# An earlier first AV in a fused attention and GELU kernel, with a weight load and a key load issued ahead of the weighing of v

## The chip, the cores and the metric

One core of one Trainium2 chip. The metric is the device time of one execution in microseconds (us); a "run" is one timed execution. Engines are named as in the profile: PE = TensorE, DVE = VectorE, ACT = ScalarE, POOL = GpSimd, SP = SyncE (which here only issues DMAs). The granted clock is the share of full speed at which the profile shows TensorE's clock; a load lands when its last byte has arrived. AV is the product of the exps with v.

## The reference

Attention with a decay that depends on `f`, over 8 batches of 8 heads (576 rows of 64), and then two matrix products with an exact GELU between them.

```python
def _attn_ref(q, k, v, f):                      # q, k, v: (8, 8, 576, 64)
    scores = scale * np.matmul(q, k.transpose(0, 1, 3, 2))
    cum = np.cumsum(np.log(np.clip(f, 0.0001, 1.0)), axis=-1)
    scores = np.where(causal, -1e9, scores + cum[:, :, :, None] - cum[:, :, None, :])
    ... softmax ...
    return np.matmul(attn, v)
def _moe_ref(x, w_in, w_out):                   # x: (4608, 512), d_ff = 2048
    h = x @ w_in
    return (0.5 * h * (1.0 + erf(h / sqrt(2)))) @ w_out
```

## The kernel before

The program is scheduled by hand: each engine executes its instructions in the order of the code. Batch 0's attention comes first, then its product with `w_in` (the "GEMM stream", line L385). Batch 1's attention follows, with parts of batch 0's `w_out` product (L517) as filler, and so on for each batch. Three jobs lie on GpSimd: it issues the loads of q, k, `w_in` and `w_out` (they convert to bf16), multiplies v by the decay ("weighing", four calls a batch, one for each pair of heads), and cuts the causal triangle out of the exps ("masks"). v is loaded by SyncE, batch 1's in two halves of four heads and five pieces each.

```python
def load_v(b, h0=0, h1=H):                       # L119, SyncE's queue
    for n in range(NBLK):
        p0 = D if n == NBLK - 1 else 0
        nc.sync.dma_start(v_sb[p0:P, h0:h1, n, :], v[b, h0:h1, ...])
def load_w_out(c):                               # L175, GpSimd's queue
    nc.gpsimd.dma_start(w_out_sb[:, kt, :], w_out_r[:, kt, :])
def weigh_v(b, i, eng=nc.gpsimd):                # L268: vw = v * w, heads 2i, 2i+1
    eng.tensor_tensor(vw(b)[:, hs, :, 0:D], v_sb[:, hs, :, :], w..., Alu.mult)
def scores(b, i, t):                             # L299 matmuls, then
    nc.scalar.activation(et[:, :, z:c], st[:, :, z:c], Act.Exp, scale=scale)   # L309
    for c0 in [] if on_pe else SDIAG[t]:         # on_pe: batch 0, and pair 0 of batch 1
        nc.gpsimd.affine_select(...)             # L311, a mask
# attend(b, i, h): AV, L330.   gemm1: the stream on w_in, L385.
# ... cut ...
def second_attention():                          # batch 1
    weigh_v(1, 2)
    weigh_v(1, 3)
    for i in range(HP):
        for t in range(4):
            scores(b, i, t)
            # ... transposes of q and k (i == 0), w_out filler (i > 1) ...
            if i and t in (1, 2):
                av(i - 1, t - 1)
            if (i, t) == (1, 3):
                load_qk_tokens(2, which="k")
    # ... cut ...
    load_w_out(2); load_w_out(3)
    load_v(2)
# in batch 0's GEMM stream:
if ffb == 12:
    weigh_v(1, 0)
    load_w_out(0); load_w_out(1)
    weigh_v(1, 1)
    load_qk_tokens(2, which="q")
```

The softmax here doesn't subtract the row's maximum and nothing guards it: scores larger than these inputs give would overflow.

## Time and profile before

| | before |
|---|---|
| time, first three runs | 344.74 us (343.18 to 345.57) |
| time, with the three runs beside the changed kernel | 343.41 us (342.94 to 345.57) |
| span of the profiled execution, granted clock | 343.5 us, 0.996 |
| long GEMM streams of batch 0 and 1 start | 25.60, 59.41 us |
| first AV of batch 2; last stream of matmuls starts | 84.49, 323.94 us |

A timeline line is: start, length, engine, line of the code, operation, output and inputs, and in brackets the idle time before and what ended it. These are GpSimd's weighings of batch 1, the w_out issue between them, and then TensorE's AV of batch 1's second pair and its GEMM stream:

```profile
39.42 1.28 POOL L268 TENSOR_TENSOR vw<-v_sb,wT 128x640 bf16<-128x640 f32 x1 [12.60 <-DMA v_sb<-in_v_dram]
40.79 1.56 POOL L175 DMA_DIRECT2D w_out_sb<-in_moe_w_out_dram  x2
...
44.58 1.29 POOL L268 TENSOR_TENSOR vw<-v_sb,wT 128x640 bf16<-128x640 f32 x1
```
```profile
49.18 0.64 PE L330 MATMUL o<-vw,e 128*128 128x65 bf16 x15
...
59.41 13.21 PE L385 MATMUL ps<-xT,w_in_sb 128*128 128x512 bf16 x60
```

The third weighing, at 44.58, has no bracket: GpSimd came to it without waiting. It reads v's second half, whose last piece the chain of waits shows (start, length, what):

```profile
36.90 4.98 DMA v_sb<-in_v_dram
```

It was issued at 36.90 and landed at 41.88, so 2.7 us before it was needed.

### The profile page before, as it was taken

The numbers are of one execution on the slowest core, as the hardware profiler recorded it, in microseconds if no ns is written. First come the engines' busy times: TensorE is split into PE (matmuls) and PEld (weight loads), VectorE is DVE, ScalarE is ACT, GpSimd is POOL, SyncE is SP. The second block draws the span as 40 slices with busy tenths as digits, with TensorE's granted clock in tenths as the row PEclk, the third lists the DMA queues.
The fourth block names the chain that finished last, engine by engine and source line by source line (L and its number), as shares of the span: only waits on it lengthen the run. The fifth ranks groups of instructions, "written<-read, shape, count | busy, mean of one in ns | idle before, by whom it ended". The sixth has DMA issues, their size and how long they took to land.

```text
span 343.5 us, 7832 instructions
## 1 busy us (share of the span) xinstructions
PE 332.4 (97%) x3172; PEld 172.6 (50%) x3172; DVE 184.7 (54%) x417; ACT 210.3 (61%) x299; POOL 121.9 (35%) x247
## 2 busy tenths in 40 slices
PE   8799999999999999999999999999999999999993
PEld 3574555445554456445644564456544654444442
DVE  4670355664457935796479646964696450010021
ACT  6986786773643787368737873787378746305500
POOL 8180492208634244623454343624352420000000
PEclk9999999999999999999999999999999999999998
DMA  8999999995998999398949698679900240020022
GB/s 117 177 175 194 160 178 129 134 210 119 220 200 207 140 180 199 101 137 125 232 121 132 117 200 168 86 132 205 164 31 2 88 85 31 0 93 32 0 61 63
DMA packets 104628, 44.18 MB, mean 129 GB/s; under 512 B 83408, under 2 KB 100048, under 8 KB 104592
## 3 DMA queue, kind: packets, MB, share of 16 engines
q1 hardware_dynamic: 87296, 29.52, 44.8%
q0 software_dynamic: 16896, 13.63, 27.5%
q8 instruction: 25, 0.41, 0.5%
q10 hardware_dynamic: 400, 0.52, 0.4%
q14 instruction: 11, 0.09, 0.1%
HBM read 36.85 MB, written 9.44 MB: 135 GB/s over the span
## 4 chain that ended last, share of the span: by engine, by line
PE 72%; SPq 11%; DMA 7%; POOL 6%; issue 1%; DVE 1%; POOLq 0%
PE ps L385 28%; PE ps L479 24%; SPq L119 9%; PE ps L421 8%; PE o L330 7%; PE s L299 5%; DMA v_sb<-in_v_dram 3%; DMA k<-in_k_dram 3%; POOL vw L268 2%; SPq L235 2%; POOL q L107 1%; POOL e L311 1%; DMA xT<-x 1%; POOL k L107 1%; DVE x L344 0%
## 5 line engine op out<-in xcount | busy, mean ns | idle before, releaser
L405 ACT ACTIVATE g<-ps 128x512 bf16<-128x512 f32 x144 | 82.1, 601 | 82.2 <-PE ps L385 82.0
L309 ACT ACTIVATE e<-s 128x896 bf16<-128x896 f32 (+2 forms) x128 | 101.2, 835 | 27.4 <-PE s L299 25.4
L385 PE MATMUL ps<-xT,w_in_sb 128*128 128x512 bf16 x512 | 112.7, 379 | 0.2 <-DMA xT<-x 0.2
L479 PE MATMUL ps<-w_out_sb,g 64*128 64x512 bf16 (+1 forms) x736 | 108.5, 377 | 0.0
L385 PEld LDWEIGHTS <-w_in_sb 128*128 128x128 bf16 x576 | 55.9, 98 | 68.0 <-issue 2.3
L311 POOL TENSOR_SCALAR_AFFINE_SELECT e<-e 128x256 bf16<-128x256 bf16 (+1 forms) x135 | 49.0, 383 | 90.6 <-ACT e L309 90.1
L479 PEld LDWEIGHTS <-g 64*128 64x128 bf16 (+1 forms) x736 | 41.9, 95 | 39.7 <-issue 8.9
L268 POOL TENSOR_TENSOR vw<-v_sb,wT 128x640 bf16<-128x640 f32 x30 | 39.2, 1308 | 37.4 <-DMA v_sb<-in_v_dram 29.2
L299 PE MATMUL s<-qT,kT 64*128 64x320 bf16 (+4 forms) x384 | 45.8, 277 | 3.7 <-ACT e L309 3.2
L249 DVE COPY qT<-tq 64x288 bf16<-64x288 bf16 x96 | 42.2, 440 | 4.0 <-DMA tq<-q 2.6
L249 DVE COPY kT<-tk 64x288 bf16<-64x288 bf16 x96 | 40.9, 426 | 4.9 <-DMA tk<-k 3.4
L487 DVE COPY ot<-ps 128x512 f32<-128x512 f32 x25 | 17.3, 691 | 41.7 <-PE ps L479 41.7
L330 PEld LDWEIGHTS <-e 128*128 128x128 bf16 x960 | 34.4, 98 | 7.4 <-POOL e L311 3.0
L330 PE MATMUL o<-vw,e 128*128 128x65 bf16 x960 | 37.3, 194 | 0.2 <-POOL e L311 0.2
L344 DVE TENSOR_TENSOR x<-o,r 128x320 bf16<-128x320 f32 x64 | 31.5, 491 | 2.2
L430 DVE COPY ot<-ps 128x512 f32<-128x512 f32 (+2 forms) x9 | 5.7, 633 | 48.9 <-PE ps L421 48.9
L299 PEld LDWEIGHTS <-kT 64*128 64x128 bf16 x384 | 19.6, 94 | 23.8 <-issue 10.5
L421 PE MATMUL ps<-w_out_sb,g 128*128 128x512 bf16 (+2 forms) x144 | 28.0, 356 | 0.0
L343 DVE RECIPROCAL r<-o 128x5 f32<-128x5 f32 x64 | 12.1, 190 | 22.8 <-PE o L330 22.6
L421 PEld LDWEIGHTS <-g 128*128 128x128 bf16 x144 | 13.5, 98 | 14.5
L490 DVE TENSOR_TENSOR ot<-ot,ps 128x512 f32<-128x512 f32 x25 | 17.2, 687 | 1.4
L216 DVE COPY qT<-ps_f 128x576 bf16<-128x576 bf16 x7 | 5.3, 754 | 17.3 <-PE ps_f L207 17.3
(64 smaller groups left out, 147.3 us busy)
## 6 DMA issues: line engine op xcount, KB each, us to landing
out_dram<-ot SPq DMA_DIRECT2D x32, 256.0 KB, 2.6
v_sb<-in_v_dram SPq DMA_DIRECT2D x24, 256.0 KB, 5.2
q<-in_q_dram POOLq DMA_DIRECT2D x6, 576.0 KB, 6.1
k<-in_k_dram POOLq DMA_DIRECT2D x6, 576.0 KB, 8.1
v_sb<-in_v_dram SPq DMA_DIRECT2D x22, 128.0 KB, 5.5
w_in_sb<-in_moe_w_in_dram POOLq DMA_DIRECT2D x4, 512.0 KB, 7.9
w_out_sb<-in_moe_w_out_dram POOLq DMA_DIRECT2D x4, 512.0 KB, 8.4
q<-in_q_dram POOLq DMA_DIRECT2D x4, 144.0 KB, 4.4
```

Of the source, the lines that this page charges most:

```text
L119: nc.sync.dma_start(v_sb[p0:P, h0:h1, n, :], v[b, h0:h1, K0[n] + p0 : K0[n] + P].rearrange("h p d -> p h d"),)
L249: nc.vector.tensor_copy(rows[:, odd], src[odd * D : (odd + 1) * D, 2 * i + h].rearrange("d j p -> d p j"),)
L268: eng.tensor_tensor(vw(b)[:, hs, :, 0:D], v_sb[:, hs, :, :], w.unsqueeze(3).to_broadcast([P, 2, NBLK, D]), Alu.mult,)
L299: nc.tensor.matmul(to, *ab, start=half < 0, stop=half == 1 or not masked)
L309: nc.scalar.activation(et[:, :, z:c], st[:, :, z:c], Act.Exp, scale=scale)
L311: nc.gpsimd.affine_select(out=et[:, :, c0 + z : c0 + P], in_=et[:, :, c0 + z : c0 + P], compare_op=Alu.is_ge, fill=0.0, base=z, pattern=[[ ...
L330: nc.tensor.matmul(o[:, m, :], e_of[b, i, t][:, h, c : c + P], vw_of[b][:, 2 * i + h, n, :], start=(n == 0), stop=(n == m),)
L344: nc.vector.tensor_tensor(x_of[b, i][:, :, h, :], o[:, :, 0:D], r.unsqueeze(2).to_broadcast([P, NBLK, D]), Alu.mult,)
L385: nc.tensor.matmul(ps, w_in_sb[:, kt, ffb * P : (ffb + 1) * P], src[:, kt, 0:TC], start=(kt == 0), stop=(kt == n_dm - 1),)
L405: nc.scalar.activation(g_of[c][ffb], ps, Act.Gelu)
L421: nc.tensor.matmul(pss[ts][:, c0:c1], g_of[c][kt][:, ts * P : (ts + 1) * P], w_out_sb[:, kt, c0:c1], start=(kt == 0), stop=(kt == n_ff - 1),)
L479: nc.tensor.matmul(banks[r], g_of[c][kt][rows, ts * P : (ts + 1) * P], w_out_sb[rows, kt, :], start=kt == (steps.index("r") if r else 0), ...
```

## The change

Its intent: keep TensorE busy in batch 0's attention by mixing the part that ScalarE paces with the part that TensorE paces, and bring batch 1's and batch 2's data in early enough for the time gained. Part 1 changes only the order in the first attention (one 128x640 copy goes from ScalarE to VectorE). Part 2 moves loads: w_out's first half behind a gate on a piece of v's first half and ahead of the first weighing, k of batch 2 next to q, and w_out's second half ahead of the end of batch 1's scores. A gate is a GpSimd copy of 64x1 out of a piece of v: GpSimd waits in it until that piece has landed, and so does all that follows it in GpSimd's order.

```diff
+    def gate(h, n):
+        t = x_pool.tile([P, 1], FP32, tag="gate", name="gate")
+        nc.gpsimd.tensor_copy(t[D:P], v_sb[D:P, h, n, 0:1])
 # part 1: first_attention (cut)
-        for t in (1, 2, 3):
-            scores(0, 1, t)
+        scores(0, 1, 1)
+        scores(0, 1, 2)
+        transposes_first(0, 3, 0, m_psum, "m")
+        scores(0, 1, 3)
+        transposes_first(0, 3, 1, m_psum, "m")
+        weigh_v(0, 0, nc.vector)
+        weigh_v(0, 1, nc.vector)
+        gate(0, 4)
-        scores(0, 2, 0)          # and the transposes and weighings, now above
-        for t in range(4):
-            scores(0, 3, t)
-            attend_head(*divmod(t, 2))
+        for i, t in ((2, 2), (2, 3), (3, 0), (3, 1), (3, 2), (3, 3)):
+            scores(0, i, t)
+            attend_head(*heads.pop(0))
 # part 2: second_attention, and batch 0's stream
-                if (i, t) == (1, 3):
-                    load_qk_tokens(2, which="k")
+                if (i, t) == (3, 3):
+                    load_w_out(2)
+                    load_w_out(3)
-        load_w_out(2)
-        load_w_out(3)
         load_v(2)
                 if ffb == 12:
-                    weigh_v(1, 0)
+                    gate(0, 2)
                     load_w_out(0)
                     load_w_out(1)
+                    weigh_v(1, 0)
                     weigh_v(1, 1)
-                    load_qk_tokens(2, which="q")
+                    load_qk_tokens(2)
```

More of the change, by code (lines that the diff above doesn't have):

```diff
@@ L576, in first_attention @@
         transposes(2, m_psum, "m")
-        for t in (1, 2, 3):
-            scores(0, 1, t)
-        gate = x_pool.tile([P, 1], FP32, tag="gate", name="gate")
-        nc.gpsimd.tensor_copy(gate[D:P], v_sb[D:P, 0, 4, 0:1])
+        scores(0, 1, 1)
[6 more added lines that the diff above has]
+        gate(0, 4)
         load_w_in(0)
@@ L584, in first_attention @@
         weigh_v(0, 3)
-        scores(0, 2, 0)
-        transposes_first(0, 3, 0, m_psum, "m")
-        scores(0, 2, 1)
-        transposes_first(0, 3, 1, m_psum, "m")
-        weigh_v(0, 0, nc.vector)
-        weigh_v(0, 1, nc.vector)
         load_w_in(2)
@@ L597, in first_attention @@
         load_qk_tokens(1, 4, 8)
-        scores(0, 2, 2)
-        scores(0, 2, 3)
-        for t in range(4):
-            scores(0, 3, t)
-            attend_head(*divmod(t, 2))
-        attend_head(2, 0)
-        to_xT(0, 0, nc.scalar.copy)
-        attend_head(2, 1)
+        scores(0, 2, 0)
+        scores(0, 2, 1)
+        heads = [(i, h) for i in range(3) for h in range(2)]
+        for i, t in ((2, 2), (2, 3), (3, 0), (3, 1), (3, 2), (3, 3)):
+            scores(0, i, t)
+            attend_head(*heads.pop(0))
+        to_xT(0, 0, nc.vector.tensor_copy)
         to_xT(0, 1, nc.scalar.copy)
```

## The prediction

> **What bounds the kernel now.** I read the page's busy line first, then TensorE's timeline of the first 110 us with its idle times, then ScalarE's and GpSimd's timelines beside it, and the chain of work that ended last.
>
> ```profile
> PE 332.4 (97%) x3172; PEld 172.6 (50%) x3172; DVE 184.7 (54%) x417; ACT 210.3 (61%) x299; POOL 121.9 (35%) x247
> ```
>
> TensorE (PE) is busy for 97% of a 343.5 us span and nothing else passes 61%. From 86 us on the chain is TensorE almost alone, and the change touches nothing there, so those 257 us stay and arrive earlier or later as a block. What can be won lies in front of 86 us, and is at most TensorE's idle and stalled time there. The first attention is one such place. These are its lines in TensorE's timeline (start, length, what, and in brackets the idle time before it), then the exps in ScalarE's:
>
> ```profile
> 10.93 0.29 PE L299 MATMUL s<-qT,kT 64*128 64x256 bf16 x2 [0.40 <-ACT e L309]
> 13.41 0.31 PE L299 MATMUL s<-qT,kT 64*128 64x320 bf16 x2 [0.49 <-ACT e L309]
> 14.22 0.29 PE L299 MATMUL s<-qT,kT 64*128 64x256 bf16 x2 [0.41 <-ACT e L309]
> 17.42 0.28 PE L299 MATMUL s<-qT,kT 64*128 64x256 bf16 x2 [0.56 <-ACT e L309]
> ...
> 20.64 1.28 PE L330 MATMUL o<-vw,e 128*128 128x65 bf16 x30
> ...
> 25.31 0.45 PE L363 MATMUL ps_x<-key_of,x 128*128 128x128 bf16 x5
> 25.60 12.35 PE L385 MATMUL ps<-xT,w_in_sb 128*128 128x512 bf16 x56
> ```
> ```profile
> 8.48 11.21 ACT L309 ACTIVATE e<-s 128x896 bf16<-128x896 f32 x14
> 19.84 1.61 ACT L309 ACTIVATE e<-s 128x896 bf16<-128x896 f32 x2 [0.15 <-PE s L299]
> ```
>
> The reader is to see two regimes: until about 17.4 us ScalarE's 16 exps set the pace (some 0.8 us each, back to back) and TensorE waits for a score buffer; after that TensorE is saturated, with four heads of AV left over behind the last exp (20.64 to 24.4), until the long GEMM stream at 25.60. Further on, GpSimd (POOL) sets TensorE's time twice:
>
> ```profile
> 47.34 1.72 POOL L311 TENSOR_SCALAR_AFFINE_SELECT e<-e 128x256 bf16<-128x256 bf16 x5
> 49.01 0.82 POOL L107 DMA_DIRECT2D k<-in_k_dram  x1
> ```
> ```profile
> 73.94 4.64 DMA v_sb<-in_v_dram
> 78.75 1.28 POOL vw L268
> 80.20 1.21 POOL vw L268
> 81.58 0.76 POOL q L107
> 82.33 0.76 POOL k L107
> 83.10 1.73 POOL e L311 x5
> 84.88 0.97 PE o L330 x25
> ```
>
> The first is GpSimd's timeline: the five masks of batch 1's second pair end at 49.0, and TensorE starts the AV that reads them at 49.18, so there is only some 0.2 us of slack. The second is the chain: batch 2's v lands at 78.7, its weighing, the issue of batch 3's q and k and five masks follow, and TensorE's AV stalls for it (30 matmuls take 1.36 us at 84.49, 1.11 us at 90.03: 0.25 us lost). The same chain runs back through the transposes of batch 2's k to its load, issued at 49.01 and landed at 58.3.
>
> **What the Trainium skill says.** Perfetto Trace Analysis, section "Optimization Strategy": where the most contended engine changes over time, interleave the regimes. That is the first part of the change, and the trace agrees that there are two (ScalarE's to 17.4 us, TensorE's after). SBUF — State Buffer, section "Who interferes with whom": a VectorE instruction with two SBUF inputs contends with a GpSimd instruction that reads SBUF, and the second to issue blocks. The trace agrees: GpSimd's first weighing, beside VectorE's at 17.56, took 1.87 us, and 1.28 us elsewhere. DMA: Bandwidth & Descriptors, section "Queues, rings and completion order": the engines round-robin between queue rows and take one ring's descriptors in order. So I take q, k, w_in and w_out (all from GpSimd's queue) as one line, beside v and the transposes (SyncE's). The landings fit: w_out at 46.5 and 48.7, q at 53.5, k at 58.3.
>
> **Part 1, the first attention.** No work is added or removed: it is the order, and one 128x640 copy (0.7 us on ScalarE, 0.49 on VectorE) changes engine. I replay TensorE with the durations of the timeline: scores 0.46, 0.30, 0.38 and 0.33 us for the four tiles, a transpose group 0.49, a head's AV 0.58 between scores, 0.56 otherwise, xT 0.3; a score may start 0.16 after the exp before last has gone (17.42 after 17.26), and an exp starts 0.45 after its scores.
> - The transposes of the last pair (2 x 0.49) go to 12.9 and 13.74. They fill the idle 0.49 and 0.41 there; the scores at 13.41 and 14.22 keep their places.
> - The first score of pair 2 stays at 14.22, the second goes to 14.95, the third waits for an exp until 15.76 and ends at 16.14.
> - The first AV needs VectorE's weighing. v lands at 15.4 (issued 8.20, 7.2 to landing; GpSimd's gate on it fires at 15.50), VectorE is free by 15.1, a weighing takes 0.82: so AV at 16.35, after 0.2 us of waiting.
> - Then six pairs of score and AV, 0.95 us each: scores at 16.93, 17.84, 18.88, 19.76 and 20.72. The exps slip: the last starts at 21.17 (20.75 before) and ends at 21.87.
> - Behind: AV of pair 2's second head to 21.61, two xT to 22.25, AV to 22.81, xT, AV to 23.66, four GEMM matmuls to 24.52, and the last xT 0.98 after the last AV as before: 24.64 against 25.31.
> So part 1 brings the GEMM stream forward by **0.67 us**: the 1.46 us of idle that it fills, less the 0.8 or so that it newly waits ahead of and after pair 2's scores.
>
> **Part 2, the loads.** Alone, part 1 would be lost at both of GpSimd's pins. Between v's landing (39.24) and the first mask GpSimd has now: four weighings with their casts 5.6 us, two w_out issues 1.56, one q issue 0.83, sum 7.99, which is 47.3. The change puts w_out behind a gate on an earlier piece of v (its third piece lands at 35.0), so 1.56 goes, and k's issue (0.82) comes in: the masks start 0.74 earlier, 46.55, and end at 48.3. TensorE, 0.67 ahead, wants them at 48.51. It fits. k of batch 2 is then issued near 43.2 in place of 49.0; w_out starts in the idle DMA stretch (40 to 44 us: mean busy share 0.48), lands some 4 us earlier, and q and k take 4.8 us each behind it: k lands at 54.6 (estimate) against 58.3. SyncE's transposes and v follow it, so v of batch 2 lands near 75 against 78.7. w_out's second half, issued at 56.5 in place of 60.5, takes some of that. Three microseconds are left, more than the 0.67 needed, and the stall of **0.25 us** at 84.5 goes too.
> Sum: 0.67 + 0.25 = 0.92 us at best.
>
> **The rivals.**
> - GpSimd is blocked by VectorE's weighing. Gate and weighing now wait for the same landing at 15.4, both read SBUF, and VectorE is idle. If it goes first, w_in's issue comes 0.8 us later, and with it the whole saturated stretch of DMA up to batch 1's v at 39.24 (now 40.0). The masks then end at 49.0 and TensorE stalls 0.5 us there: the gain is 0.2 + 0.25, time 344.3. Against it: the second weighing on VectorE no longer delays GpSimd's own (0.6 us back). About even with the main line.
> - v stays late. w_out and k move only from one end of a saturated queue to the other (DMA share 1.1 to 1.5 from 44 to 56 us), v of batch 2 does not come earlier, and the pin at 84.9 holds: nothing gained, 344.7. Against it is the idle DMA at 40 to 44 and 58 to 60 us.
> - The w_out loads, issued while batch 1's q, k and v still come in (landings 37.7 to 41.9), delay them; the transposes at 41.5 would wait. One to two microseconds lost, 346. Against it: one ring in order, so w_out stands behind q and k.
> - More is won: AV and scores overlap better than in my replay, all 1.46 us are saved and the stall too: 343.0.
>
> **Range and chances.** Mean of main line (0.9) and first rival (0.45), with the tails on both sides nearly even: 0.7 to 0.8 us off 344.74, so 343.9. Single runs of before lie between 343.18 and 345.57, so a median of few runs moves by about a microsecond by itself; hence 342.5 to 345.0. Two per cent is 6.9 us, more than TensorE's whole idle time before 86 us (88 less 82.7, 5.3 us), so faster is nearly ruled out; slower would need a stall several times any I see. Chances: faster 0.01, same 0.98, slower 0.01.
>
> **What would show it.** The gap of 0.56 at 17.42 and those of 0.49 and 0.41 gone; the first AV near 16.35; the last exp's end near 21.9; the GEMM stream's start near 24.9; w_in's issue at 15.96 (main line) or 16.8 (first rival); batch 1's masks ending before 48.5, without a wait of TensorE; k landing before 56, v of batch 2 before 76; no stall in the first AV of batch 2; the stretch from there to the end equal to before. A GEMM stream earlier by 0.6 with the same end would prove me wrong on part 2; a start at 25.3 or later, on part 1.

## More of the kernel before

A weighing of pair 0 or 1 reads the first half, of pair 2 or 3 the second.

In the view of the DMA queues from 36 to 40 us, q1 is SyncE's queue and q0 GpSimd's; the columns are packets, MB and the time their packets took as a share of 16 engines (packets overlap, so a sum over 100% is possible):

```profile
q1 hardware_dynamic: 2226, 0.55, 71.9%
q0 software_dynamic: 472, 0.34, 54.1%
```

w_out is not yet issued in this stretch, and v (q1) gets the larger part of the engines.

## The result, and the profile after

All outputs are correct. Each ratio in this document is the mean time of one kernel's fast runs over the mean of the other's from the same rounds, so it is not quite the ratio of the medians quoted.

| | before | after |
|---|---|---|
| median of six runs | 343.41 us (342.94 to 345.57) | 348.84 us (345.93 to 350.55) |
| ratio, 95% interval | | 1.0137 (1.0088 to 1.0186) |
| long GEMM stream of batch 0 starts | 25.60 | 24.68 |
| AV of batch 1's second pair (bulk of it) | 49.18 | 53.10 |
| long GEMM stream of batch 1 starts | 59.41 | 65.44 |
| first AV of batch 2 | 84.49 | 90.53 |
| last stream of matmuls starts | 323.94 | 329.59 |

The change cost some 5 us instead of winning 0.8. TensorE's timeline after:

```profile
24.68 12.35 PE L385 MATMUL ps<-xT,w_in_sb 128*128 128x512 bf16 x56
...
52.14 0.29 PE L330 MATMUL o<-vw,e 128*128 128x65 bf16 x2 [3.67 <-POOL e L311]
53.10 1.09 PE L330 MATMUL o<-vw,e 128*128 128x65 bf16 x13 [0.67 <-POOL e L311]
...
65.44 13.21 PE L385 MATMUL ps<-xT,w_in_sb 128*128 128x512 bf16 x60
...
90.53 1.11 PE L330 MATMUL o<-vw,e 128*128 128x65 bf16 x30
```

Two things are new. TensorE is idle for 3.67 and 0.67 us, waiting for GpSimd's masks. And behind the wait the matmuls are slow: 13 AV matmuls take 1.09 us, where 15 took 0.64. The account of the profiled executions, by the table above: +3.92 us up to the AV (0.92 gained in front already counted in), +2.11 from there to the GEMM stream (12.34 us against 10.23), +0.01 in the stream, and -0.39 behind batch 2's first AV, 0.25 of it the stall that the prediction wanted gone (30 matmuls now take 1.11 us, not 1.36). The sum is 5.65, close to the 5.43 between the medians.

Why the masks are late, in GpSimd's timeline after:

```profile
36.82 0.18 POOL L546 COPY gate<-v_sb 64x1 f32<-64x1 f32 x1 [10.93 <-DMA v_sb<-in_v_dram]
37.29 1.50 POOL L175 DMA_DIRECT2D w_out_sb<-in_moe_w_out_dram  x2 [0.28 <-issue]
...
44.46 0.78 POOL L107 DMA_DIRECT2D k<-in_k_dram  x1
48.93 1.28 POOL L268 TENSOR_TENSOR vw<-v_sb,wT 128x640 bf16<-128x640 f32 x1 [3.68 <-DMA v_sb<-in_v_dram]
...
51.68 2.68 POOL L311 TENSOR_SCALAR_AFFINE_SELECT e<-e 128x256 bf16<-128x256 bf16 x8
```

w_out is issued at 37.29, 3.5 us earlier than before. The third weighing, which never waited, now waits 3.68 us for v's second half, and the masks stand behind it in GpSimd's order. The masked pair itself does not need that half: the AV at 52.14 is of pair 1, whose v was weighed by the second weighing. The chain of waits names the piece:

```profile
38.56 10.21 DMA v_sb<-in_v_dram
```

The same 64 KB piece took 4.98 us before and takes 10.21 us now; it was also issued 1.66 us later, and lands at 48.77 in place of 41.88. The DMA queues from 40 to 44 us, after:

```profile
q0 software_dynamic: 597, 0.59, 89.2%
q1 hardware_dynamic: 977, 0.24, 32.8%
```

GpSimd's queue (w_out, then q) takes most of the engines' time with packets of about 1 KB (0.59 MB in 597), and v's packets of about 0.25 KB (0.24 MB in 977) move at less than half of the 0.55 MB in 4 us that they reached before.

The slow matmuls behind the wait are seen in the windows of 2 us. Columns: stretch, length, busy time and instructions of PE, PEld, DVE, ACT and POOL, granted clock of TensorE, DMA share, GB/s:

```profile
52.00:54.00 2.00, 1.18 (x15) 0.86 (x15) 0.00 (x0) 0.00 (x0) 2.00 (x7) 0.50 1.15 148
54.00:56.00 2.00, 2.00 (x18) 0.97 (x16) 0.69 (x2) 0.92 (x1) 0.60 (x3) 0.50 0.59 106
56.00:58.00 2.00, 2.00 (x17) 0.67 (x14) 0.69 (x2) 0.70 (x1) 0.45 (x2) 0.50 0.97 175
```

The granted clock is 0.50 from about 51.2 to 58.0 us; before, it is 1.00 throughout this stretch. Before and after:

```profile
52.00:54.00 2.00, 2.00 (x28) 1.14 (x25) 0.62 (x2) 1.70 (x3) 1.12 (x3) 1.00 1.12 160
```
```profile
48.00:50.00 2.00, 0.46 (x2) 0.00 (x0) 0.18 (x1) 0.86 (x2) 1.07 (x1) 1.00 1.31 206
50.00:52.00 2.00, 0.00 (x0) 0.00 (x0) 0.00 (x0) 0.00 (x0) 2.00 (x5) 0.80 1.33 205
```

The Trainium skill, TensorE: Matmul & The Clock Gate, section "What's actually happening", says that the clock halves after an idle window of about 3.4 us and comes back after about as much busy time. This trace agrees only in part. (A mean of 0.80 from 50 to 52 is full clock until 51.2 and half clock after; windows of 0.25 us say the same.) The half clock lasted 6.8 us, twice that window. But it began some 2.75 us after the end of the last matmul (48.46) and before the masks came: less idle time was enough. What it cost is read best against part1_only and wout_late (below), whose AV comes in the same two parts at full clock: from the 13 matmuls to the GEMM stream they take 10.44 us, the change 12.34. So 1.90 of the 2.11 us go with the clock.

The times of the runs fit, but they don't prove it. The changed kernel was timed twice, six runs each. In nine runs the mean clock was 0.990 to 0.995 and the time 348.31 to 350.55 us (mean 349.1); in three it was 0.999 or 1.000, and the time 345.93, 346.47 and 344.95 us (mean 345.8). How long TensorE waited in those three is not known, as only one execution of each call was profiled: a shorter wait would give a shorter time and leave the clock up as well.

### The profile page after: what moved, and what is told of

The parts are those of the page before. It is cut to its first block, busy times and chain, and to the rows that moved or that the text cites. A ratio compares the mean times of both kernels' runs of the same rounds, so it can differ in the third digit from the quotient of the medians.

```text
span 347.3 us, 7835 instructions
## 1 busy us (share of the span) xinstructions
PE 334.9 (96%) x3172; PEld 173.8 (50%) x3172; DVE 187.0 (54%) x418; ACT 209.6 (60%) x298; POOL 122.2 (35%) x248
## 4 chain that ended last, share of the span: by engine, by line
PE 83%; SPq 5%; DMA 5%; POOL 3%; DVE 1%; issue 1%; ACT 0%; POOLq 0%; DVEq 0%; ACTq 0%
PE ps L385 32%; PE ps L479 27%; PE ps L421 8%; PE o L330 8%; PE s L299 6%; SPq L119 5%; DMA v_sb<-in_v_dram 5%; PE ps L517 2%; POOL vw L268 1%; POOL q L107 1%; POOL e L311 0%; POOL k L107 0%; DVE vw L268 0%; DVE x L344 0%; POOL w_in_sb L171 0%
## 5 line engine op out<-in xcount | busy, mean ns | idle before, releaser
L479 PEld LDWEIGHTS <-g 64*128 64x128 bf16 (+1 forms) x736 | 41.9, 94 | 40.2 <-issue 9.3
L268 POOL TENSOR_TENSOR vw<-v_sb,wT 128x640 bf16<-128x640 f32 x30 | 38.5, 1286 | 20.0 <-DMA v_sb<-in_v_dram 11.4
L249 DVE COPY kT<-tk 64x288 bf16<-64x288 bf16 x96 | 42.1, 439 | 1.6
L330 PE MATMUL o<-vw,e 128*128 128x65 bf16 x960 | 38.2, 195 | 4.5 <-POOL e L311 4.5
L385 PE MATMUL ps<-tails,w_in_sb 128*128 128x512 bf16 x64 | 14.3, 377 | 0.0
```

Of the source, the lines that this page charges most:

```text
L249: nc.vector.tensor_copy(rows[:, odd], src[odd * D : (odd + 1) * D, 2 * i + h].rearrange("d j p -> d p j"),)
L330: nc.tensor.matmul(o[:, m, :], e_of[b, i, t][:, h, c : c + P], vw_of[b][:, 2 * i + h, n, :], start=(n == 0), stop=(n == m),)
L385: nc.tensor.matmul(ps, w_in_sb[:, kt, ffb * P : (ffb + 1) * P], src[:, kt, 0:TC], start=(kt == 0), stop=(kt == n_dm - 1),)
L479: nc.tensor.matmul(banks[r], g_of[c][kt][rows, ts * P : (ts + 1) * P], w_out_sb[rows, kt, :], start=kt == (steps.index("r") if r else 0), ...
```

## The experiments

The letters that the expectations use for the theories, where the argument needs them: A, w_out issued ahead of the weighing takes DMA engines from v's second half; B, it is the early k of batch 2; C, part 1 delays v by itself, by the gate that VectorE's weighing blocks; D, the late loads themselves hold TensorE up; E, the fall of the clock adds about 2 us to the wait; F, it costs nothing; G, it is q and k together; H, the order of masks and weighings alone wins. Diffs are against the changed kernel unless another is named. Each call of several kernels went to one chip, with its own runs of the kernel before, so ratios count and not medians of different calls. Overview (call, median, ratio to before with interval, and from the one profiled execution of each the last landing of v's second half and the start of the last matmul stream, 323.94 before and 329.59 after):

| kernel | call | us | ratio (95%) | v lands | last stream |
|---|---|---|---|---|---|
| part1_only | 1 | 343.85 | 1.0004 (0.9979 to 1.0029) | 42.3 | 323.78 |
| part2_only | 1 | 345.93 | 1.0063 (1.0021 to 1.0105) | 45.7 | 325.04 |
| wout_late | 1 | 343.88 | 1.0003 (0.9961 to 1.0044) | 41.0 | 322.98 |
| k_late | 1 | 348.99 | 1.0161 (1.0098 to 1.0224) | 47.3 | 327.91 |
| masks_first | 2 | 342.54 | 0.9959 (0.9929 to 0.9989) | 47.9 | 322.68 |
| spread | 2 | 343.55 | 0.9988 (0.9953 to 1.0023) | 42.3 | 323.17 |
| warm_wait | 2 | 347.98 | 1.0120 (1.0079 to 1.0161) | 46.6 | 328.91 |
| qk_after_v | 2 | 349.37 | 1.0159 (1.0121 to 1.0198) | 48.4 | 330.10 |
| after_again | 3 | 348.90 | 1.0139 (1.0097 to 1.0181) | 48.1 | 328.83 |
| warm_again | 3 | 348.22 | 1.0146 (1.0115 to 1.0177) | 48.2 | 330.32 |
| before_masks | 3 | 343.43 | 1.0011 (0.9984 to 1.0038) | 42.9 | 323.63 |
| part1_masks | 3 | 343.22 | 0.9997 (0.9969 to 1.0024) | 43.8 | 323.92 |
| warm12 | 4 | 346.54 | 1.0082 (1.0040 to 1.0124) | 47.6 | 327.37 |
| masks_again | 4 | 342.97 | 0.9971 (0.9941 to 1.0000) | 48.2 | 322.56 |

**part1_only: the change without part 2.**

```diff
                 if ffb == 12:
-                    gate(0, 2)
+                    weigh_v(1, 0)
                     load_w_out(0)
                     load_w_out(1)
-                    weigh_v(1, 0)
                     weigh_v(1, 1)
-                    load_qk_tokens(2)
+                    load_qk_tokens(2, which="q")
 # load_w_out(2), (3) and k of batch 2 back where they were
```

> The kernel before with part 1 alone (order of the first attention), all loads as before. Theory A (w_out, issued ahead of the weighings, takes the DMA from the second half of batch 1's v): v's last piece lands near 42 to 43 us as before (41.9), the GEMM stream of batch 0 starts near 24.7, but the masks of batch 1's second pair still end near 49.0 and TensorE, 0.9 us early, waits for them up to 0.9 us: time 0 to 0.9 us below before. Rival B (q and k together are what delays v): the same as A here. Rival C (part 1 itself delays v, by the GpSimd gate that VectorE's weighing blocks, 0.85 us in place of 0.19): v's last piece later than 45 us, time 3 to 5 us over before.

The time is that of before. In the trace the GEMM stream starts at 25.01 (0.59 earlier), the masks at 47.80 (0.46 later than before), TensorE waits 0.39 us for them, and batch 1's stream starts at 59.65: the gain is gone at the masks, as the prediction said of part 1 alone. Part 1 alone gave neither a late v (42.3) nor a wait of several us. But C's own mechanism was not in this execution: its gate took 0.18 us, not 0.85. Two later traces settle C. In spread the gate took 0.85 us and v still landed at 42.3; in after_again it took 0.18 us and v landed at 48.1. C falls.

**part2_only: before with part 2 alone.**

```diff
 # against before
                 if ffb == 12:
+                    gate(0, 2)
                     load_w_out(0)
                     load_w_out(1)
+                    weigh_v(1, 0)
                     weigh_v(1, 1)
-                    load_qk_tokens(2, which="q")
+                    load_qk_tokens(2)
 # and the other lines of part 2
```

> The kernel before with part 2 alone (gate on v's third piece, w_out ahead of the weighings, q and k of batch 2 together, w_out's second half earlier), the first attention as before. A and B: v's last piece lands at 47 to 49 us, TensorE waits 3 to 4 us for masks at 49 and its granted clock falls for some microseconds: 4.5 to 6.5 us over before. C: within 1 us of before.

Slower, but by 2.1 us only: a miss in size. The third weighing waited 2.31 us, yet TensorE's AV at 50.90 waited for nothing, because TensorE came to it late. Its batch-0 GEMM stream started only at 27.32: in this execution VectorE's two weighings of batch 0, beside GpSimd's, took 3.76 us (1.56 in the changed kernel). So the wait was hidden behind another loss. Of its four runs two had clock 0.998 or 1.000 (344.76 and 344.81 us) and two 0.995 (347.04 and 347.59), so in two the clock fell all the same, at a place that no trace shows.

**wout_late: the change with w_out where it was, behind the first weighing.**

```diff
-                    gate(0, 2)
+                    weigh_v(1, 0)
                     load_w_out(0)
                     load_w_out(1)
-                    weigh_v(1, 0)
                     weigh_v(1, 1)
                     load_qk_tokens(2)
```

> The changed kernel without the second gate, w_out's first half issued after the first weighing as before; q and k still together, the rest as changed. A: v's last piece lands before 44 us, TensorE's wait for masks is below 1 us, no fall of the clock, time 0 to 1.2 us below before. B: v's last piece still after 46 us, time 3 us or more over before. C: as B.

The loss is gone. v's last piece takes 5.09 us and lands at 41.0, the masks start at 47.00, the wait is 0.38 us, batch 1's stream starts at 58.85 and batch 2's first AV has no stall. All other moves of the change are in this kernel, so the place of the w_out issue (with its gate) is necessary for the loss. The last stream starts 0.96 us earlier than before, near the gain that was predicted; the time does not show it (1.0003, with an interval of 1.4 us on either side).

**k_late: the change with k of batch 2 where it was.**

```diff
-                    load_qk_tokens(2)
+                    load_qk_tokens(2, which="q")
+                if (i, t) == (1, 3):
+                    load_qk_tokens(2, which="k")
```

> The changed kernel with batch 2's k issued in the second attention as before, w_out still ahead of the weighings. A: v's last piece still lands after 46 us, TensorE still waits over 2.5 us, time 4 to 5.5 us over before. B: v's last piece before 44 us and the time within 1 us of before.

As slow as the change: v's last piece takes 9.61 us, TensorE waits 2.14 and 0.73 us, and the granted clock falls to 0.50 behind that. B falls.

**qk_after_v: q and k of batch 2 issued behind the third weighing.** Now w_out alone shares the engines with v.

```diff
                 if ffb == 12:
                     ...
-                    load_qk_tokens(2)
         weigh_v(1, 2)
+        load_qk_tokens(2)
         weigh_v(1, 3)
```

> The changed kernel with batch 2's q and k both issued behind the third weighing, which waits for v's last piece, so that only w_out can compete with v. Theory A (w_out alone is enough): v's last piece lands after 45.5 us and the time is still 2.5 us or more over before. Rival G (w_out and q together are needed): v's last piece before 44.5, time under 1.5 us over before.

v's piece took 10.35 us, and TensorE's timeline shows the longest wait of all:

```profile
53.34 0.29 PE L330 MATMUL o<-vw,e 128*128 128x65 bf16 x2 [5.23 <-POOL e L311]
```

G falls, and w_out alone is enough. With wout_late, A is settled: the w_out loads double the time of v's piece, whatever q and k do.

**masks_first: the change with the third and fourth weighing behind the masks.** The loads stay as changed. This tests whether the late v itself costs anything, or only the masks' place behind it.

```diff
-        weigh_v(1, 2)
-        weigh_v(1, 3)
         for i in range(HP):
             for t in range(4):
                 scores(b, i, t)
+                if (i, t) in ((1, 3), (2, 3)):
+                    weigh_v(1, i + 1)
```

> The changed kernel with the weighings of batch 1's third and fourth pair moved behind the masks of its second and third pair in GpSimd's order; all loads stay where the change put them. Theory A (w_out ahead starves v, and what TensorE waits for is the masks that stand behind the weighings): v's last piece still lands at 47 to 49 us, but the first AV of the second pair waits under 0.5 us and the third pair's under 1.5 us, no loss of clock: time within 1 us of before. Rival D (the late loads themselves, or the transposes of q and k that follow, hold TensorE up): the wait only moves and the time stays 3 us or more over before.

GpSimd's and TensorE's timelines of masks_first:

```profile
45.01 1.01 POOL L311 TENSOR_SCALAR_AFFINE_SELECT e<-e 128x256 bf16<-128x256 bf16 x3 [0.60 <-ACT e L309]
...
48.41 1.28 POOL L268 TENSOR_TENSOR vw<-v_sb,wT 128x640 bf16<-128x640 f32 x1 [0.89 <-DMA v_sb<-in_v_dram]
```
```profile
48.33 0.64 PE L330 MATMUL o<-vw,e 128*128 128x65 bf16 x15
...
58.55 13.21 PE L385 MATMUL ps<-xT,w_in_sb 128*128 128x512 bf16 x59
```

v is as late as in the change (the third weighing still waits for it, until 48.41), but the masks start at 45.01 and wait for exps instead, and the AV starts at 48.33 without a wait, 0.85 before its time in the kernel before. The last stream starts 1.26 us earlier than before. D falls. The time is 0.41% below before's (1.4 us), with the interval below 1: faster than the kernel before, and by the ratios than the change. **masks_again** repeated it:

> masks_first once more. A: 0.7 to 1.6 us below before, as in its first run (1.4 by the ratio) and in its trace (last TensorE stream 1.3 us earlier). If the first run was luck: within 0.4 us of before.

0.9971, last stream at 322.56. The two agree: some 0.3 to 0.4% under before, though the second interval reaches 1.

**spread: masks_first with w_out behind the first weighing.** It combines the two cures.

```diff
 # against masks_first
-                    gate(0, 2)
+                    weigh_v(1, 0)
                     load_w_out(0)
                     load_w_out(1)
-                    weigh_v(1, 0)
                     weigh_v(1, 1)
```

> As masks_first, and w_out's first half issued after the first weighing as before. A: v's last piece before 44 us, masks of the second pair end before 48, no wait of TensorE for them over 0.3 us, long GEMM stream of batch 1 about 0.9 us ahead of before (59.4), no stall in batch 2's first AV: 0.8 to 1.3 us below before. D: no better than 0.3 us below.

A miss: no gain to be seen in the time. The trace shows a wait that takes the place of the one removed:

```profile
47.24 0.38 PE L517 MATMUL ps<-w_out_sb,g 128*128 128x512 bf16 x1 [0.96 <-DMA w_out_sb<-in_moe_w_out_dram]
```

TensorE's filler needs w_out at 46.3, and a load issued at 41.43 is not there yet. The early w_out of the change serves a purpose once the front has become faster.

With masks_first, spread also answers whether v's own late issue (1.66 us in the change) makes v late. In the two profiled executions the last piece was issued at 37.68 and 37.66 us, and the place of w_out, with its gate, is the only difference in the code. KB and us to landing, masks_first and then spread:

```profile
v_sb<-in_v_dram SPq DMA_DIRECT2D x1, 64.0 KB, 10.2
```
```profile
v_sb<-in_v_dram SPq DMA_DIRECT2D x1, 64.0 KB, 4.6
```

And in after_again the piece was issued at 36.37, earlier than in the kernel before, and took 11.74 us. The late issue is not the cause.

**before_masks and part1_masks: the new order of the masks on the kernel before, and on part1_only.** (The edit is that of masks_first.)

> The kernel before with nothing changed but GpSimd's order (third and fourth weighing of batch 1 behind the masks). A says that the masks are not what holds the kernel before up (slack of 0.2 us), so nothing is gained: within 0.4 us of before. Rival H (the gain of masks_first is the order of masks alone, the change has no part in it): 1 us or more below before.

> The first attention of the change and GpSimd's new order, all loads as before. If part 1 and the order of masks are all that is needed: as masks_first, 1.2 to 1.6 us below before. If w_out ahead is needed too (in spread TensorE waited 0.96 us for w_out near 47 us): TensorE waits for w_out near 47 to 48 us, batch 2's first AV still stalls for late v, 0 to 0.8 us below before.

Neither differs from before. H falls. In part1_masks TensorE waits 0.61 us for w_out at 48.03, as in spread. Of the kernels with part 1, only the one that has the early w_out and the masks' new order as well (masks_first) shows no wait of TensorE before this AV.

**warm_wait, warm_again, warm12: the change with filler matmuls ahead of the AV that waits** (20, 20 and 12 of them, on a zero tile, results unused). They keep TensorE busy in the wait and should keep its clock.

```diff
+                if (i, t) == (2, 1):
+                    psk = o_psum.tile([P, TC], FP32, tag="o", name="ps_k")
+                    for _ in range(20):          # 12 in warm12
+                        nc.tensor.matmul(psk, warm[:, 0:P], warm, start=True, stop=True)
                 if i and t in (1, 2):
                     av(i - 1, t - 1)
```

> The changed kernel with 20 needless matmuls (about 4.3 us at full clock) put on TensorE just ahead of the AV that waits for masks, result unused. Theory E (part of the loss is the granted clock, which falls when TensorE has idled some microseconds): the clock stays at 1.0 through 50 to 60 us, the mean is 0.998 or more in most runs, and the time is 1.5 to 2.5 us below the changed kernel's, 346 to 347. Rival F (the fall costs nothing, the wait is all): time as the changed kernel's, 348 to 349.

The clock stayed at 1.00 in the profiled execution, and the stretch from the AV to the GEMM stream took 10.23 us (53.18 to 63.41) as before the change, in place of 12.34. But the time was 347.98, outside what E expected and at the edge of what F did: the 20 matmuls take about 4.3 us, as long as the wait itself, and the profiled execution had another wait of 1.16 us at 181 us. So it was run again, beside the change:

> The changed kernel once more, so that the next run can be set against it on the same chip. Theories A and E: 4.5 to 6 us over before, mean clock 0.99 to 0.995 in most runs; a run in which the clock does not fall is some 2 us shorter.

> warm_wait again, beside the changed kernel on the same chip (its first run was set against the changed kernel of another chip job, and the profiled execution had a wait of 1.2 us for a transpose near 181 us that has nothing to do with it). E (the fall of the clock costs time of its own): mean clock 0.998 or more, 1 to 2.5 us below after_again. F (it costs nothing): within 0.5 us of after_again.

The change repeated (1.0139). warm_again was no faster (1.0146), which is the outcome for F, although five of its six runs kept a mean clock of 0.998 or more. Those five have a mean of 347.9 us; the two full-clock runs of after_again took 346.47 and 344.95. So a full clock alone did not bring the time back, and why is open: the fillers may cost what they save in executions in which v comes earlier. The profiled execution is no guide to the five, being the one run at 0.990. Its clock stayed at 1.00 in the wait for masks, but had been 0.50 from 14.6 to 21.5 us, in the first attention, behind a wait of 1.71 us for a load of k; its GEMM stream started at 28.03. A mean clock, then, does not tell where the clock fell. With 12 fillers, shorter than the wait:

> As warm_wait with 12 matmuls (about 2.6 us) in place of 20, so that they end before the masks do and cost nothing by themselves. E (the clock's fall costs about 2 us): granted clock 1.0 from 50 to 60 us, mean 0.998 or more in most runs, 2 to 4 us over before (the changed kernel was 4.8 over). F (it costs nothing): 4.5 us or more over before, whatever the clock.

The windows of warm12 beside the wait (the last column but two is the granted clock):

```profile
54.00:56.00 2.00, 2.00 (x23) 0.86 (x19) 0.69 (x2) 1.53 (x3) 0.81 (x2) 1.00 0.70 135
56.00:58.00 2.00, 2.00 (x28) 1.12 (x27) 1.59 (x4) 1.33 (x3) 1.06 (x3) 1.00 1.03 187
```

The clock is 1.00 throughout, although v still lands at 47.6 and TensorE still waits; the GEMM stream starts at 62.41. (That is 3.03 us before the change's, but 1.13 of them are an AV that came earlier, 51.97 for 53.10.) The time is 1.0082 of before: 2.8 us lost, where the change loses 4.7 to 4.8 (1.0137 and 1.0139). Four of its six runs (clock 0.998 to 1.0) lie at 345.60 to 347.29, two (0.990 and 0.995) at 348.42 and 348.52. This supports E, but the intervals overlap, it was another chip, and warm_again speaks against it. What is shown is the cost in TensorE's timeline: from the bulk of the AV to the GEMM stream 12.34 us (the change), 12.26 (after_again), 11.87 (k_late) and 11.61 (qk_after_v) where the clock fell, 10.23 (warm_wait, warm_again) and 10.44 (warm12) where it did not. How much of it is left in the device time is not shown.

## Why the prediction was wrong

**Part 1 was right, and won more than was said.** The long GEMM stream started at 24.68, 0.92 earlier; the prediction had 0.67, which is 24.9. (The 24.64 and 25.31 of its replay are starts of the last xT, which came at 24.39.) The rest fits: first AV at 16.45 (16.35), the last exp's end at 21.95 (21.87), gaps of 0.49, 0.41 and 0.56 gone, one of 0.64 new at 16.05. The first rival came half true, in GpSimd's timeline after:

```profile
15.58 0.85 POOL L546 COPY gate<-v_sb 64x1 f32<-64x1 f32 x1 [7.32 <-DMA v_sb<-in_v_dram]
```

The gate took 0.85 us where it had taken 0.19, beside VectorE's weighing, and w_in was issued at 16.37, between the 15.96 and the 16.8 named. That alone did no harm: in spread the gate took 0.85 us too, and v landed at 42.3. In after_again, the same code as the change, the gate took 0.18 us, so this delay comes in some executions only.

**Part 2 failed at one step: "the masks start 0.74 earlier, 46.55".** The sum of GpSimd's own work between v's landing and the first mask was worked out right (less 1.56, plus 0.82), on the ground that GpSimd is bound by its own instructions there. But 39.24 us was only the landing of v's *first* half. Weighings three and four read the second half, which had landed at 41.88, with 2.7 us to spare, and the prediction took the four as one block without asking what each waits for, although the 41.9 stands in its third rival. With the spare gone, the block has a wait of 3.68 us in it, and the masks start at 51.68, not 46.55.

**The rival that came true was dismissed with a wrong reason.** The third rival named the mechanism (w_out delays what is still coming in) and a loss of one to two microseconds. It was set aside with "one ring in order, so w_out stands behind q and k". That is true of q and k, which share GpSimd's queue. It says nothing of v, which the prediction itself had put on SyncE's queue "beside" that line. The rival also had the wrong reader wait: the transposes, at 41.28, waited 0.19 us for k; it was the third weighing that waited, 3.68 us. The rule cited there, that the engines alternate between queues, points the other way for v: w_out's packets and v's take turns. The Trainium skill says the same in DMA: Bandwidth & Descriptors, section "Issuing engines are not separate DMA queues": DMAs from different engines run on the same 16 DMA engines and interleave. The trace agrees: 0.24 MB of v in 4 us beside w_out and q, 0.55 MB without w_out.

**Its size was too small as well.** Even taken up, the rival said 346. The wait alone makes more than that in the trace: +3.92 us at the AV, less the 0.39 won back later, is 3.5. What was not thought of is the clock: in the trace it adds 1.90 us behind the wait.

**What held besides.** k of batch 2 landed at 54.6 (54.6), batch 2's v by 72.3 (75), the stall of 0.25 us is gone, and the stretch from batch 2's second AV to the last stream of matmuls changed by 0.14 us only. The w_out loads landed at 45.6 and 49.0, not "some 4 us earlier". Before, they landed at 46.53 and 50.05; the prediction's 48.7 was misread (issued at 41.60, the second took 8.45 us; 7.1 is the median of the two). Issued 3.5 us earlier, they took 8.3 and 11.0 us, so the move bought little even for w_out itself.

**The chances.** "Same", to within 2%, had 0.98 and is what was measured (1.4%), but with the wrong sign: the width of the class held, not the reasoning. "Slower would need a stall several times any I see" treated the stalls of the trace as the measure of possible stalls. The right measure was the slack (2.7 us for v) against the size of the loads moved in front of it (two of 512 KB).

**Open.** How large the clock's part is in the device time: the trace has 1.90 us, warm12 points to about 2, warm_again to nothing. Why masks_first is faster in time and wout_late is not, although their last streams start 0.3 us apart: the noise of the timing can hide it.

## What to carry to other kernels

When a load is moved forward, list what is still in flight at that moment on *every* queue, and for each its slack before its first reader; a different queue is no protection, since the engines are shared (here 5.0 us became 10.2). On an engine with an ordered queue, put work that depends on a late transfer behind work that does not: moving two instructions turned a loss of 1.4% into a gain of 0.4% here, with the late transfer still late. And a wait on TensorE can be dearer than it is long, because the clock may fall behind it (here 1.90 us in the trace).

## What the Trainium skill lacked or had wrong

- DMA: Bandwidth & Descriptors (sections "Queues, rings and completion order" and "Issuing engines are not separate DMA queues") says that engines alternate between queues by packet and that DMAs interleave, but not how unequal the shares get where packets differ in size. Here, from 40 to 44 us, 597 packets of GpSimd's queue moved 0.59 MB and 977 of SyncE's 0.24 MB, and a 64 KB piece of v took 10.2 us in place of 5.0.
- TensorE: Matmul & The Clock Gate (section "What's actually happening") gives an idle window of about 3.4 us as the condition. Here less was enough: the clock fell 2.75 us after the last matmul in the change, 2.13 in after_again, 2.47 in qk_after_v, and 0.9 in warm_again. In k_late no idle time was longer than 2.14 us (2.14 and 0.73, with two short matmuls of AV between), and it fell when TensorE had been back at work for 0.9 us. How little work in a window counts as idle is not said.
- SBUF — State Buffer (section "Who interferes with whom") says that the one of VectorE and GpSimd that issues second is blocked, and quotes slowdowns of 6.8 and 1.5 times, but none for these instructions. Here GpSimd's copy of 64x1 went from 0.19 to 0.85 us when VectorE's weighing had started 0.02 us ahead of it, and VectorE's two weighings from 1.56 to 3.76 us when GpSimd's had started 0.02 us ahead (part2_only).
